# One-core attention with routed experts: route in pieces over the next batch, a new order of the attention steps, the first expert's split on GpSimd, and six shared PSUM banks

## The chip, the cores and the metric

The kernel runs on one core of a Trainium2 chip. The metric is the device time of one execution in microseconds. The engines are TensorE (PE, with its weight loads PEld), VectorE (DVE), ScalarE (ACT), GpSimd (POOL) and SyncE (SP), which here only issues DMAs. Each takes its own instructions in order and waits on semaphores.

## The reference

Attention over 8 batches, 8 heads, 576 positions and head size 64, with a bias that depends on the position; the result, 4608 tokens of 512 values, goes through a layer of 8 experts of which each token takes one.

```python
scores = scale * np.matmul(q, k.transpose(0, 1, 3, 2)) + bias      # bias: a small net of the relative position
attn = np.exp(scores - max); attn = attn / (np.sum(attn, axis=-1, keepdims=True) + 1e-09)
x = np.matmul(attn, v)                                             # as (4608, 512)
logits = x @ w_gate; expert_idx = np.argmax(logits, axis=1); gate_w = softmax(logits)[expert_idx]
for e in range(E):
    h = np.maximum(x[expert_idx == e] @ w1[e], 0.0)
    out[expert_idx == e] = gate_w * (h @ w2[e])
```

With the inputs of this case the experts get 0, 1728, 638, 0, 1090, 576, 576 and 0 tokens. Expert 1 has the most, after six batches as after seven.

## The kernel before

**Attention.** The heads of a batch form four pairs; a pair's 576 query rows are five tiles (four of 128 rows, a tail of 64). The first ten tiles run while the bias is still built. The other 150 are steps of a list that `attend_units` writes out by hand: each operation of a step gets a key, the step's number plus an offset from the tables `LATER` and `PRODUCTS`, and all are sorted by key and issued in that order under `manual_schedule`, so the order of PE, DVE and ACT is fixed by these tables. A step is: `scores` (PE, twelve matmuls into two PSUM tiles of the pool `ps_s`, which has two), `biased` (DVE, one for each head: adds the bias and finds the row minimum), `weights` (ACT, the exponential, whose row sums go to the tile `r`), `turn` (PE transposes, in two parts, each into two of the three tiles of the pool `ps_t`) and `turned` (copies to SBUF, part on ACT, part on DVE). Tiles are joined to units, [0, 1] and [2, 3, 4] of a pair. For a unit follow `values` (PE, five pieces of four matmul instructions into the single tile of `ps_o`), `values_out` (ACT), `rows` (PE, turns back and forms the gate's logits, in a `ps_t` tile), `divided` (DVE, 1e-9 and reciprocal of the sums) and `rows_out` (DVE, scales rows and logits out of the `ps_t` tile). For the next pairs `first_part` (ACT) and `second_part` (DVE) split q and k in a high and a low half. The last two pairs run as ten units of one tile each.

**Route.** Once a batch is through, `route` (a generator with seven yields and so eight pieces) picks each token's expert, counts ranks (on GpSimd, then two pairs of matmuls), and scatters the rows to DRAM by GpSimd's indirect DMAs. `advance(1)` runs one piece; the list has one in every step.

**Experts.** `first_expert` picks the fullest expert so far; `load_first` reads its first weights; `split_first` splits them in high and low halves (four chunks, high by a DVE cast, low by a GpSimd subtraction) and loads the second weights into the same raw tiles. The first block of 384 tokens (`tokens`, `first_product`) starts at the end of the attention. `run` then splits the second weights (ACT, DVE) and goes through the experts; each runs one arm of a switch, with blocks of up to 384 tokens. A block is `first_product` (PE at line 705, ACT relu at 695, DVE low half at 696, PSUM tiles from `ps_h`, three) and `second_product` (lines 741 to 743, DVE at 745, indirect DMA at 746, PSUM tiles from `ps_y`, three). `fetch` loads the next expert's eight chunks, w1 in the chunks 0 to 3 and w2 in 4 to 7, and splits w2 on GpSimd. Outside the hand-written order a planner with a model of the costs sets the order in each engine.

Of the kernel before, what the change touches and what calls it, by code (L numbers as in the profile page):

```python
# [48 lines left out]
    "S": 0.000, "St": 0.040, "W0": 0.497, "W1": 0.498, "Wt": 0.839, "X0": 0.575, "X1": 1.291, "Xt": 0.930,  # L49
    "R1": 1.085, "R2": 1.921, "R1t": 1.872, "E1a": 1.506, "E1b": 1.546, "E2a": 1.922, "E2b": 1.937, "E1at": 2.076,  # L50
    "E1bt": 2.107, "hi0": 1.250, "lo0": 4.000, "hi1": -0.245, "lo1": 1.364, "raw": -2.445, "v": -2.500, "route": -0.261,
}
PRODUCTS = {
    "two": ((2.690, 2.691, 4.592, 4.689, 4.690), 4.691, 6.523, 2.285, 6.524),
    "three": ((2.108, 2.109, 2.110, 2.111, 3.123), 3.548, 5.123, 2.096, 5.923),
    "one": ((2.700,) * 5, 2.800, 4.133, 4.033, 4.933),
}
AW = max(sum(QN[qt] for qt in qts) for qts in UNITS)
LEAD, RATE = 15, 4

# [27 lines left out]
def attention(tc, ctx, q, kt, vm, ltab, bcst, gate, gt, cm, cmat, ival, tail0, pcst, bias, xs, plan, moe):  # L88
# [154 lines left out]

    def divided(un):

        r, m, tail = un["r"], 2 * len(un["qts"]), QN[un["qts"][-1]] < P
        nc.vector.tensor_scalar(out=r[:, :m - tail], in0=r[:, :m - tail], scalar1=1e-9, scalar2=None, op0=ALU.add)
        nc.vector.reciprocal(out=r[:, :m - tail], in_=r[:, :m - tail])
        if tail:
            nc.vector.tensor_copy(out=r[:64, m - 1:m], in_=r[64:, m - 2:m - 1])  # L250
# [41 lines left out]
    for t in r_tiles:  # L292
        nc.gpsimd.memset(t, 0.0)
    r_tiles = itertools.cycle(r_tiles)

    def attend(b, pr, qt):
# [18 lines left out]
        with tc.manual_schedule(engines=PE):  # L315
            rows(un)
        divided(un)
        rows_out(un)

    def attend_units(units, ops):  # L320
# [8 lines left out]
        for b, pr, qts in units:  # L329
# [3 lines left out]
            for i, (qt, st) in enumerate(zip(qts, sts)):  # L333
# [24 lines left out]
                at(k + LATER["route"], lambda: advance(1))  # L358
            when, o, x, d, y = PRODUCTS[("one", "two", "three")[len(qts) - 1]]
# [4 lines left out]
            at(last + x, lambda un=un: rows(un))  # L364
            at(last + d, lambda un=un: divided(un))
            at(last + y, lambda un=un: rows_out(un))
            if pr == NPAIR - 1 and qts[-1] == QT - 1:
                at(last + y + .01, lambda b=b: pending.append(route(b)))
            if p not in begun:
                begun.append(p)  # L370
# [26 lines left out]
    def route(b):  # L397
# [42 lines left out]
        nc.scalar.activation(out=lg, in_=lg, func=AF.Exp)  # L440
        g = rp_.tile([P, QT], F32, name="g")
# [164 lines left out]
    ops += [((B - 1, 3, 4), key, token_part) for key in (-2., 2.953, 2.963, 2.973, 2.983)]  # L606
# [14 lines left out]
class Experts:  # L621
# [163 lines left out]
    def run(self, ctx):  # L785
# [17 lines left out]
        for c in range(NC):  # L803
            self.split(NC + c, 0, raw=self.wraw[c])
# [129 lines left out]
```

## Time and profile before

| | us |
|---|---|
| median of three runs | 1101.14 (1099.69 to 1104.77) |
| the profiled execution, own time | 1104.94 |
| its span, first to last instruction | 1103.0 |
| mean granted TensorE clock | 0.967 |
| PE, DVE, ACT, POOL busy | 1008.5, 653.7, 560.9, 172.0 |

The span has a stage of attention with the bias being built (to about 107 us), a long even stage of attention (to 534 us), the last two pairs (to 602 us), the first block of the first expert (to 642 us), the rest of the experts (to 1082 us) and an end of 20.6 us after the last matmul. Times in the profile are microseconds from the start of the span, and a line number is that of the listing above. A matmul's end is modelled, so neighbours overlap; the distance between two starts tells the pace.

### The profile page before, as it was taken

The page shows a single profiled execution, that of the slowest core. Times are in us where ns is not written, and L with a number is a line of the kernel's source. Part 1 is how long each engine was busy: PE and PEld are TensorE (multiplying, and loading weights), DVE is VectorE, ACT ScalarE, POOL GpSimd, SP SyncE. Part 2 cuts the span into 40 slices and gives each one's busy share as a digit, 9 for nine tenths or more (in the row PEclk, how much of TensorE's full clock was granted, in tenths as well). Part 3 has the DMA queues.
Part 4 walks back from the last instruction along what each step waited for, and adds up shares of the span by engine and source line. Part 5 has one row for each costly group of instructions (what it writes and reads, how often), then busy time and mean ns, then how long its engine had stood idle before and what let it go on. Part 6 is the DMA issues. An engine that isn't in the chain of part 4 may idle for free. (4 is left out here: it accounts for less than half of the span.)

```text
span 1103.0 us, 24830 instructions
## 1 busy us (share of the span) xinstructions
PE 1008.5 (91%) x9564; PEld 799.5 (72%) x9564; DVE 653.7 (59%) x1794; ACT 560.9 (51%) x1371; POOL 172.0 (16%) x235
## 2 busy tenths in 40 slices
PE   7888899999999999999995999999898999898892
PEld 3445676777777776767674888889787899786791
DVE  7677588888888888888887523224232323223140
ACT  6776587888888887878864111113122123022130
POOL 0000002002020202011032224000410500151320
PEclk9899799999999999999998899999999999999896
DMA  8444122223232323223133273003416102606000
GB/s 246 120 110 98 46 61 93 80 60 114 60 103 70 104 71 102 64 63 107 49 133 106 70 280 117 24 27 106 162 49 243 49 10 83 211 23 205 36 20 30
DMA packets 39046, 104.89 MB, mean 95 GB/s; under 512 B 4835, under 2 KB 5347, under 8 KB 38755
## 3 DMA queue, kind: packets, MB, share of 16 engines
q1 hardware_dynamic: 32642, 83.01, 24.7%
q0 software_dynamic: 5920, 18.95, 4.7%
q8 instruction: 91, 1.49, 0.6%
q14 instruction: 105, 0.85, 0.2%
q10 hardware_dynamic: 288, 0.59, 0.2%
HBM read 72.97 MB, written 23.97 MB: 88 GB/s over the span
## 5 line engine op out<-in xcount | busy, mean ns | idle before, releaser
L190 ACT ACTIVATE a<-t,mn 128x576 f32<-128x576 f32 x288 | 224.2, 778 | 62.9 <-DVE mn L182 59.4
L705 PE MATMUL psh<-bias,bias 128*128 128x384 f32 (+2 forms) x1248 | 207.8, 323 | 22.1 <-issue 13.5
L182 DVE CUSTOM_DVE_ANT_0 t<-s,bias 128x576 f32<-128x576 f32 x288 | 207.6, 753 | 32.5 <-PE s L173 26.8
L705 PEld LDWEIGHTS psh<-bias,bias 128*128 128x128 f32 x1248 | 198.8, 195 | 29.1 <-issue 15.2
L228 PE MATMUL o<-at,v 128*64 128x256 f32 (+3 forms) x1520 | 186.3, 380 | 14.6 <-DVE at L215 12.7
L695 ACT ACTIVATE bias<-psh 128x384 fp32r<-128x384 f32 (+2 forms) x104 | 46.5, 451 | 263.8 <-PE psh L705 263.5
L207 PEld LDWEIGHTS tps<-cm,a 64*128 64x128 f32 (+1 forms) x2624 | 116.6, 140 | 70.6 <-issue 34.8
L207 PE MATMUL tps<-cm,a 64*128 64x64 f32 (+1 forms) x2624 | 147.5, 233 | 11.5 <-DVE at L218 8.7
L228 PEld LDWEIGHTS o<-at,v 128*64 128x64 f32 x1520 | 92.5, 138 | 63.7 <-DVE at L215 12.3
L218 ACT COPY at<-tps 128x320 f32<-128x320 f32 (+1 forms) x312 | 116.4, 392 | 41.6 <-PE tps L207 37.1
L696 DVE SCALAR_TENSOR_TENSOR bias<-psh,bias 128x384 fp32r<-128x384 f32 (+2 forms) x104 | 51.6, 504 | 110.5 <-ACT bias L695 108.9
L218 DVE COPY at<-tps 128x320 f32<-128x320 f32 (+1 forms) x200 | 92.7, 464 | 26.2 <-PE tps L207 24.7
L173 PE MATMUL s<-kh,qh 64*128 64x288 f32 x512 | 95.7, 338 | 5.1 <-ACT ob L562 3.9
L741 PE MATMUL psy<-w2h,bias 128*128 128x512 f32 (+1 forms) x224 | 88.6, 398 | 0.0
L742 PE MATMUL psy<-w2l,bias 128*128 128x512 f32 (+1 forms) x224 | 88.1, 396 | 0.0
L743 PE MATMUL psy<-w2h,bias 128*128 128x512 f32 (+1 forms) x224 | 88.0, 396 | 0.0
L746 POOL DMA_INDIRECT out<-y,ids x38 | 37.3, 981 | 303.2 <-DVE y L745 270.8
L745 DVE TENSOR_SCALAR y<-psy,g 128x512 f32<-128x512 f32 (+1 forms) x38 | 28.4, 747 | 94.6 <-PE psy L743 94.6
L173 PE MATMUL s<-kh,ql 64*128 64x288 f32 x512 | 83.1, 298 | 0.0
L173 PE MATMUL s<-kl,qh 64*128 64x288 f32 x512 | 82.0, 296 | 0.0
L680 ACT CAST bias<-tps 128x384 fp32r<-128x384 f32 (+2 forms) x60 | 24.6, 461 | 87.0 <-PE tps L678 77.0
L419 POOL TENSOR_TENSOR cs<-cs,oh 128x8 f32<-128x8 f32 x40 | 8.1, 202 | 376.8 <-DVE oh L414 374.3
(168 smaller groups left out, 1511.0 us busy)
## 6 DMA issues: line engine op xcount, KB each, us to landing
bias<-in_wl SPq DMA_DIRECT2D x28, 512.0 KB, 3.4
qn<-in_q SPq DMA_DIRECT2D x32, 320.0 KB, 2.9
v<-in_vm SPq DMA_DIRECT2D x32, 320.0 KB, 3.1
wr<-in_wl SPq DMA_DIRECT2D x20, 512.0 KB, 8.3
xg<-xs SPq DMA_DIRECT2D x12, 774.0 KB, 8.9
kn<-in_kt SPq DMA_DIRECT2D x32, 288.0 KB, 2.8
bias<-ob SPq DMA_DIRECT2D x32, 288.0 KB, 3.5
xs<-in_none SPq DMA_DIRECT2D x6, 774.0 KB, 5.0
```

The costliest lines, as they stand in the source:

```text
L173: nc.tensor.matmul(ss[hh][:, hf, :SH], x[d, q0:q0 + P], y[d, hf * SH:hf * SH + SH], start=i == 0, stop=i == 2)
L182: nc.vector.tensor_tensor_reduce(out=t, in0=st["s"][hh][:, :, :SH], in1=bt.rearrange("p (a c) -> p a c", a=2), op0=ALU.add, op1=ALU.min, s ...
L190: nc.scalar.activation(out=st["a"][:, hh * S:(hh + 1) * S], in_=st["t"][hh].rearrange("p a c -> p (a c)"), func=AF.Exp, bias=st["mn"][:, h ...
L207: nc.tensor.transpose(ts[half][:m, i * 64:i * 64 + 64], a[d, k0[half]:k0[half] + m], ident[d, d])
L218: copy(out=at[:, first:first + len(places), c0 + 64 * half:c0 + 64 * half + 64], in_=t[:, :64 * len(places)].rearrange("p (c q) -> p c q", ...
L228: nc.tensor.matmul(un["o"][d, :N], v[:, c, d], at[:, c if c == 4 else 5 * hh + c, :N], start=i == 0, stop=i == 4, skip_group_check=True)
L695: nc.scalar.activation(out=hi, in_=ps, func=AF.Relu)
L696: nc.vector.scalar_tensor_tensor(out=lo, in0=ps, scalar=0.0, in1=hi.bitcast(F32), op0=ALU.max, op1=ALU.subtract)
L705: nc.tensor.matmul(ps[:, :N], w[c][:, k0:k0 + P], x[kc][:, :N], start=i + kc == 0, stop=i == 2 and kc == KC - 1)
L741: nc.tensor.matmul(ps[:n], a, wh, start=f == 0, stop=False)
L742: nc.tensor.matmul(ps[:n], a, wo, start=False, stop=False)
L743: nc.tensor.matmul(ps[:n], b, wh, start=False, stop=f == FC - 1)
```

## The change

In the attention: new offsets for all steps; the addition of 1e-9 (and the move of the tail's sum) is taken out of `divided` and becomes `raised`, on ACT; the eight pieces of a route stand two steps apart over the next batch (1.3 steps for the seventh batch), from 10.768 steps after the batch's last step, and the exponential of the route ends a piece of its own. `first_expert` now sees the counts of six batches and not of seven. The cast of `split_first` moves from DVE to GpSimd. Among the experts: `first_product` and `second_product` take their PSUM tiles from one pool of six; the low halves of the first expert's second weights are made by GpSimd and not by DVE; `fetch` loads w2 ahead of w1.

```diff
 LATER = {
-    "S": 0.000, "St": 0.040, "W0": 0.497, "W1": 0.498, "Wt": 0.839, "X0": 0.575, "X1": 1.291, "Xt": 0.930,
-    "R1": 1.085, "R2": 1.921, "R1t": 1.872, "E1a": 1.506, "E1b": 1.546, "E2a": 1.922, "E2b": 1.937, "E1at": 2.076,
-    "E1bt": 2.107, "hi0": 1.250, "lo0": 4.000, "hi1": -0.245, "lo1": 1.364, "raw": -2.445, "v": -2.500, "route": -0.261,
+    "S": 0.000, "St": 0.035, "W0": 0.570, "W1": 0.571, "Wt": 0.657, "X0": 0.784, "X1": 1.453, "Xt": 0.778,
+    "R1": 1.176, "R2": 1.888, "R1t": 1.829, "E1a": 1.528, "E1b": 1.596, "E2a": 2.425, "E2b": 2.049, "E1at": 2.290,
+    "E1bt": 2.351, "hi0": -0.113, "lo0": 1.538, "hi1": 1.359, "lo1": 2.762, "raw": -2.313, "v": -2.500, "route": 10.768,
 }
 PRODUCTS = {
-    "two": ((2.690, 2.691, 4.592, 4.689, 4.690), 4.691, 6.523, 2.285, 6.524),
-    "three": ((2.108, 2.109, 2.110, 2.111, 3.123), 3.548, 5.123, 2.096, 5.923),
-    "one": ((2.700,) * 5, 2.800, 4.133, 4.033, 4.933),
+    "two": ((2.742, 3.289, 4.079, 4.736, 4.742), 5.200, 6.742, 3.763, 5.895, 7.000),
+    "three": ((2.495, 2.768, 2.833, 3.408, 3.411), 4.004, 5.412, 3.804, 5.440, 5.933),
+    "one": ((3.014,) * 5, 3.114, 4.421, 3.104, 4.322, 4.943),
 }
+ROUTE_STEP = (2., 1.3)
+    def raised(un):
+        r, m, tail = un["r"], 2 * len(un["qts"]), QN[un["qts"][-1]] < P
+        if tail:
+            nc.scalar.activation(out=r[:64, m - 1:m], in_=r[64:, m - 2:m - 1], func=AF.Identity, bias=tiny[64:], scale=1.0)
+        nc.scalar.activation(out=r[:, :m - tail], in_=r[:, :m - tail], func=AF.Identity, bias=tiny, scale=1.0)
+
     def divided(un):
-        r, m, tail = un["r"], 2 * len(un["qts"]), QN[un["qts"][-1]] < P
-        nc.vector.tensor_scalar(out=r[:, :m - tail], in0=r[:, :m - tail], scalar1=1e-9, scalar2=None, op0=ALU.add)
-        nc.vector.reciprocal(out=r[:, :m - tail], in_=r[:, :m - tail])
-        if tail:
-            nc.vector.tensor_copy(out=r[:64, m - 1:m], in_=r[64:, m - 2:m - 1])
+        r, m = un["r"], 2 * len(un["qts"])
+        nc.vector.reciprocal(out=r[:, :m], in_=r[:, :m])
...
-                at(k + LATER["route"], lambda: advance(1))
...
                 at(last + y + .01, lambda b=b: pending.append(route(b)))
+                if b < B - 1:
+                    for i in range(8):
+                        at(last + LATER["route"] + i * ROUTE_STEP[b == B - 2], lambda: advance(1))
...
         nc.scalar.activation(out=lg, in_=lg, func=AF.Exp)
+        yield
...
-            self.split(c, None, self.nc.vector.tensor_copy, self.nc.gpsimd)
+            self.split(c, None, self.nc.gpsimd.tensor_copy, self.nc.gpsimd)
...
-            ps = self.ps_y.tile([P, DM], F32, name="psy")
+            ps = self.ps_p.tile([P, 512], F32, name="psp")
...
-                self.first_product(nt, lambda: self.ps_h.tile([P, 512], F32, name="psh"))
+                self.first_product(nt, lambda: self.ps_p.tile([P, 512], F32, name="psp"))
...
-        self.ps_h = ctx.enter_context(tc.tile_pool(name="ps_h", bufs=3, space=PSUM))
+        self.ps_p = ctx.enter_context(tc.tile_pool(name="ps_p", bufs=6, space=PSUM))
...
-        self.ps_y = ctx.enter_context(tc.tile_pool(name="ps_y", bufs=3, space=PSUM))
...
-            self.split(NC + c, 0, raw=self.wraw[c])
+            self.split(NC + c, 0, lo_by=nc.gpsimd, raw=self.wraw[c])
...
-                    for c in range(2 * NC):
+                    for c in (*range(NC, 2 * NC), *range(NC)):
```

## Rows read from the trace of the kernel before

**Rows 1.** Windows: stage, us; busy PE, PEld, DVE, ACT, POOL; clock, DMA share, GB/s.
```profile
151.06:534.33 383.27, 373.63 (x4928) 276.90 (x4929) 333.11 (x1022) 320.02 (x857) 40.37 (x96) 1.00 0.28 83
534.33:602.14 67.81, 54.96 (x776) 43.95 (x776) 54.76 (x165) 39.51 (x109) 17.48 (x19) 0.92 0.33 107
642.20:1082.40 440.20, 418.09 (x2269) 371.47 (x2267) 137.68 (x253) 87.86 (x180) 104.20 (x77) 0.98 0.29 102
```
**Rows 2.** Timeline, one pair of the even stage, PE: start us, us, operation, [idle <-releaser].
```profile
321.21 0.38 PE L173 MATMUL s<-kh,qh 64*128 64x288 f32 x2
...
323.94 0.38 PE L173 MATMUL s<-kh,qh 64*128 64x288 f32 x2
...
325.15 2.37 PE L228 MATMUL o<-at,v 128*64 128x320 f32 x16
...
327.79 0.38 PE L173 MATMUL s<-kh,qh 64*128 64x288 f32 x2
...
330.53 0.38 PE L173 MATMUL s<-kh,qh 64*128 64x288 f32 x2
...
333.24 0.40 PE L165 MATMUL s<-kh,qh 128*128 128x288 f32 x1
...
335.85 0.38 PE L173 MATMUL s<-kh,qh 64*128 64x288 f32 x2
```
**Rows 3.** Timeline, DVE: the last `rows_out` of three pairs, a route between them.
```profile
350.29 0.56 DVE L261 TENSOR_TENSOR xrow<-tps,r 128x384 f32<-128x384 f32 x1 [0.35 <-PE tps L242]
...
366.81 0.55 DVE L261 TENSOR_TENSOR xrow<-tps,r 128x384 f32<-128x384 f32 x1
...
382.32 0.56 DVE L261 TENSOR_TENSOR xrow<-tps,r 128x384 f32<-128x384 f32 x1 [0.35 <-PE tps L242]
```
**Rows 4.** Lines by form, 200 to 500 us: count | busy us, mean ns | idle before.
```profile
L247 DVE TENSOR_SCALAR r<-r 128x5 f32<-128x5 f32 x20 | 3.1, 156 | 0.0
...
L440 ACT ACTIVATE lgsum<-lgsum 128x40 f32<-128x40 f32 x5 | 1.2, 236 | 0.0
```
**Rows 5.** Timeline around the first expert's split: DVE, POOL, PE.
```profile
575.51 6.78 DVE L665 CAST bias<-bias 128x1024 fp32r<-128x1024 f32 x4
582.21 2.30 DVE L247 TENSOR_SCALAR r<-r 128x2 f32<-128x2 f32 x1
584.55 0.17 DVE L248 RECIPROCAL r<-r 128x2 f32<-128x2 f32 x1
...
576.28 10.52 POOL L666 TENSOR_TENSOR bias<-bias,bias 128x1024 fp32r<-128x1024 f32 x4 [12.37 <-DVE bias L665]
...
586.50 0.69 PE L207 MATMUL tps<-cm,a 64*128 64x64 f32 x8 [8.65 <-DVE at L218]
```
**Rows 6.** Timeline, POOL, 640 to 685 us: a later expert's split of one chunk.
```profile
663.34 1.03 POOL L665 CAST w2h3b<-wr 128x1024 fp32r<-128x1024 f32 x1
664.34 2.38 POOL L666 TENSOR_TENSOR w2l1b<-wr,w2h1b 128x1024 fp32r<-128x1024 f32 x1
```
**Rows 7.** Timeline where attention hands over to the first block: SP, PE, DVE.
```profile
587.36 0.40 SPq L673 DMA_DIRECT2D bias<-xs  x1
...
602.14 1.20 PE L678 MATMUL tps<-cm,bias 128*128 128x128 f32 x9
606.71 1.56 PE L705 MATMUL s<-bias,bias 128*128 128x384 f32 x6 [3.36 <-ACT bias L680]
...
603.47 4.63 DVE L666 TENSOR_TENSOR w2l<-bias,w2h 128x1024 fp32r<-128x1024 f32 x4 [1.80 <-ACT w2h L665]
```
**Rows 8.** The page's DMA issues: count, KB each, median us to landing.
```profile
xg<-xs SPq DMA_DIRECT2D x12, 774.0 KB, 8.9
```
**Rows 9.** Waits over the span: us in total, times, longest.
```profile
PE psh L705 <- DVE bias L696: 8.1, 4, 2.7
```
**Rows 10.** Timeline, PE, an expert's first product after a switch of arms.
```profile
779.58 6.48 PE L705 MATMUL psh<-bias,bias 128*128 128x384 f32 x36 [0.98 <-issue]
788.50 3.91 PE L705 MATMUL psh<-bias,bias 128*128 128x384 f32 x12 [2.43 <-DVE bias L696]
```

## What the rows say of the change

> **What bounds the kernel now.** I read the windows by stage first [rows 1]: the reader is to see that in the even stage of attention, 383.27 us for 25 pairs, no engine is full. DVE is busy 333.11 us (87%), ACT 320.02 (83%), and PE's 373.63 is a sum of modelled, overlapping matmuls. So the order of three nearly full engines sets the pace, and not one of them. Among the experts PE is busy 418.09 of 440.20 us at a clock of 0.98, DVE 31%: there only PE's gaps can be won. The stage between them, the last two pairs, has PE busy 54.96 of 67.81 us at a clock of 0.92.
>
> Next comes the timeline of one pair [rows 2]. Starts of scores stand at 321.21, 323.94, 327.79, 330.53, 333.24 and 335.85: a pair takes 14.64 us, in steps of 2.73, 3.85, 2.74, 2.71 and 2.61. Four steps are alike although PE has different work in them: scores fill both tiles of their pool and DVE has to read both before the next scores, and this loop is the floor. The long one is different: PE runs 16 value matmuls in it, 2.37 us without a break. Then the pairs with a route [rows 3]: 350.29 to 366.81 is 16.52 us, to 382.32 another 15.51, so 2.75 us over two plain pairs. The stage as a whole agrees: 383.27 less 25 times 14.64 (366.0) leaves 17.3 us for six routes, 2.9 each.
>
> Last, the single stalls. At 575.51 DVE begins the casts of the first expert's weights; they take 6.78 us, the small sum behind them 2.30, and PE stands 8.65 us [rows 5]. Among the experts PE waits four times, 8.1 us in all, for DVE to free a tile of the first product [rows 9].
>
> **The change part by part.** The profiled execution took 1104.94 us (span 1103.0 and 1.9 around it), 3.8 over the median of 1101.14. I sum against 1104.94 and take off 3.8 at the end.
>
> *Order of the steps.* By the new tables, PE has in the long step three pieces (12 matmuls) of the three-tile unit's values where it had four; a piece is 2.37 / 4 = 0.59 us [rows 2]. The next step has two where it had one. Of the two-tile unit's pieces the step behind that gives one to the tail's step. Long step: -0.7 (the piece and part of the wait of the transposes behind it; bounds -0.4 and -0.9). Next step: it is at the floor, so a piece costs between 0 (it fits into PE's wait) and 0.59; I take +0.3, the middle, as nothing shows PE's free time there. The two last steps: the tail's scores need one PSUM tile and not two, so the fourth can fall under the floor by up to 0.5, and the fifth gains a piece (0 to +0.5); I take -0.1 for both. Sum -0.5 us a pair, bounds -0.8 and +0.2. There are 28 pairs in the list, of which the first overlaps the bias's last stores: 27 x 0.5 = 13.5 us won, from -5 to +22.
>
> *The addition on ACT.* DVE loses a sum for each unit (0.156 us in [rows 4]) and the tail's copy, some 0.46 us a pair; ACT gains three small activations, at 0.236 at most [rows 4] 0.7 us a pair. ACT then has 320.02 / 383.27 x 14.64 + 0.7 = 12.9 of 14.1 us, so it still has room. What waits on it: only the reciprocal, which the tables put more than a step behind. Row sums come from ACT itself, so the new activation waits for nothing. I cost it at nothing beside the order above, which is what its 0.46 us on DVE makes possible; if ACT's room is gone, it costs up to 0.7 a pair, which the bound of the order takes in.
>
> *Route in pieces.* Eight pieces stood one step apart, in 1.6 pairs; they now stand two apart, in 3.2. DVE's idle time is 14.64 x 0.13 = 1.9 us a pair: 3.0 us beside the pieces before, 6.1 after, and 1.5 more for the sums taken away. Before, the ranks' matmuls also stood in PE's queue one step behind DVE's comparison and GpSimd's five sums; now two steps lie between. A piece still costs when it falls where DVE is late. I take 10 of the 17.3 us as won (bounds 0 and 17.3), and 1 of the seventh route, which moves into the single-tile units.
>
> *First split on GpSimd.* The casts leave DVE, and no DVE work there waits for them. That removes PE's 8.65 us. PE's clock of 0.92 in the stage means 0.08 / 0.5 x 67.81 = 10.8 us at 1.2 GHz, of which about 2.2 lie in work behind the stall: another 1.1. Against it: GpSimd now takes 4 x (1.03 + 2.38) = 13.6 us [rows 6] and not 10.52, though it may start on landed weights without DVE, while the second weights' and then the tokens' loads queue behind it on SP. The tokens' load was issued at 587.36 [rows 7]; by the median of 8.9 [rows 8] it lands by 596.3, and PE, 9.7 earlier, would want it at 602.14 - 9.7 = 592.4. So 0 to 3.8 us turn into a wait for that load; I take 1, since the weights' loads ahead of it make up the median. And DVE can wait for GpSimd: the third and fourth cast took most of the 6.78 us and the sum 2.30 where 0.156 is usual, all while GpSimd subtracted [rows 4, 5]; the reciprocal, 0.17, ran through. In the new order two or three of the seventh route's operations fall into the 13.6 us; 1 us. Net 7.7, from 3 to 9.7.
>
> The Trainium skill ("SBUF — State Buffer", section "SBUF: two separate sides") says that DVE, when it works over two ports or with two SBUF inputs, and GpSimd hold a shared port pair by turns, each for a whole instruction. The rows above agree for the sum (2.30 us against 0.156); the case of two SBUF inputs no row here shows. It speaks against moving work to GpSimd, and what it would do is the third rival below.
>
> *Second weights' low halves on GpSimd.* DVE was held 4.63 us from 603.47 while the tokens' low halves waited, but PE's 3.36 us at that place is ACT's [rows 7], whose casts stay. I take 1 us won, up to 3.4 if the planner also moves those casts, and down to -3 if GpSimd's 4 x 2.38 = 9.5 us, ahead of the last route's sums, holds PE at the ranks.
>
> *Six shared banks.* At 779.58 PE runs three results of 12 matmuls, 6.48 us, and stops 2.43 us because DVE is still at the switch; the next 12 take 3.91 and not 6.48 / 3 = 2.16, as the clock has fallen [rows 10]. With six tiles PE has three more results, 6.5 us, ahead: enough for the longest wait of 2.7 [rows 9]. 8.1 us for the four waits and 3 for the clock: 11 won. At worst the second product's partial results hold banks when they are wanted, and 4 remain.
>
> *w2 ahead of w1.* GpSimd, which splits w2, is busy 104.20 of 440.20 us [rows 1], and the second product wants it only a block later. Nothing, within 2 us.
>
> Sum: 13.5 + 10 + 1 + 7.7 + 1 + 11 = 44.2. 1104.9 - 44.2 = 1060.7, less 3.8: 1057 us.
>
> **The rivals.** *First, attention gains nothing (chance 0.2).* The new order only moves its waits, because the floor of 2.7 is what counts, and the route's pieces cost what they did. For it: four of five steps stand at the floor. Against: 3.85 does not. Left are 7.7 + 1 + 11: 1101.1 - 19.7 = 1081.
>
> *Second, slower (0.07).* The pool of the transposes has three tiles, and `rows` holds one until `rows_out` has read it. In the new order `rows_out` of the two-tile unit stands on DVE behind the low half of k, in a route's batch behind a piece too, and PE's next transposes want its tile. If PE stands there for 1.1 us in each pair and no route is hidden, attention is 28 x 1.1 = 31 us slower and the whole 1081 + 31 = 1112. It decides from 0.7 us a pair (19.7 / 28). Against it: DVE has 1.9 us idle a pair.
>
> *Third, the lock (0.08).* Every DVE operation with two SBUF inputs, not the sums alone, waits up to a GpSimd instruction of 2.38 us while GpSimd splits. Three in the seventh route and some four in the first block, half of it on the path: 7 x 2.38 / 2 = 8 us of the gain go, 1065. For it: the 2.30 [rows 5].
>
> *Fourth, the shared banks do not do what they say (0.03):* the planner gives them to the second product and PE still stops: 1068.
>
> **How the numbers follow.** The forecast has 0.62, 1057, its own range 1040 to 1073. The range for 8 in 10 reaches from 1040 (gains near all upper bounds, 61 us) to 1085 (the first rival and 4 us); outside lie the slower rival and some of each edge. About 0.5% is what a measurement of this kernel can tell from no change, so faster means under 1095.6: forecast, first, third and fourth rival nearly whole, 0.89; within it 0.04; slower 0.07.
>
> **What would show it.** The order: scores' starts in a plain pair with the longest step near 3.1 and a pair near 14.1. Route: pairs behind a batch's end within 0.6 us of the others. Split: no wait of PE over 4 us near the last pairs, casts at line 665 on POOL. Banks: no wait of the first product for line 696 over 0.5 us. The prediction is wrong if a pair takes 14.6 or more, if PE waits for the tokens' load by more than 4 us, or if DVE's small sums in the split's 13.6 us take over 2 us each.

## The result and the profile after

The changed kernel takes 1069.84 us (median of four runs, 1069.25 to 1071.44); the kernel before took 1100.71 on the same chip. The ratio is 0.9715, with a 95% interval from 0.9688 to 0.9742: 30.9 us won where 44 were forecast. The profiled execution took 1071.44 us, its span 1069.6, the mean clock was 0.977. Of the experiments below, those that undo one part ran on a chip like this one (before: 1100.3), but for the order of the chunks; that run and the other two groups ran on chips where the kernel before itself takes 1128.5 us, so that their times are set against before, and their stages against each other.

Line numbers are up by 12 or so: scores 174 (tail 166), transposes 208, values 229, `rows_out` 266, the route's sums 430 and ranks 434, split 677 and 678, token casts 692, first product 717, its casts and low halves 707 and 708, second product 753 to 755, its scaling 757.

**The stages.** Windows of the kernel after: even stage, last two pairs, from the tokens' transposes to the first second product, from there to the last matmul. Columns as in [rows 1].

```profile
151.02:524.40 373.38, 372.72 (x4928) 276.44 (x4928) 320.57 (x946) 334.18 (x932) 42.16 (x96) 1.00 0.27 85
524.40:591.36 66.96, 57.60 (x757) 43.79 (x757) 44.14 (x147) 40.67 (x123) 20.02 (x23) 0.95 0.32 106
591.36:617.11 25.75, 21.64 (x142) 19.18 (x140) 16.41 (x56) 10.80 (x23) 13.10 (x16) 1.00 0.03 12
617.11:1049.11 432.00, 425.81 (x2320) 378.36 (x2320) 150.09 (x267) 86.83 (x180) 106.52 (x81) 0.99 0.32 110
```

The last two stages of the kernel before, cut at the same events:

```profile
602.14:623.64 21.50, 16.79 (x87) 14.84 (x85) 13.50 (x47) 7.73 (x14) 1.01 (x5) 0.84 0.00 1
623.64:1082.40 458.76, 436.65 (x2357) 387.57 (x2356) 143.77 (x283) 89.83 (x184) 109.78 (x87) 0.98 0.30 104
```

| stage | before | after | won | forecast |
|---|---|---|---|---|
| even stage | 383.27 [rows 1] | 373.38 | 9.9 | 22.5 (order 25 x 0.5, route 10) |
| last two pairs | 67.81 [rows 1] | 66.96 | 0.9 | 9.7 (order 1, route 1, split 7.7) |
| handover and experts | 480.26 | 457.75 | 22.5 | 12 (low halves 1, banks 11) |

The sum, 33.3, is the difference of the spans within 0.1. Attention gave a third of what was forecast, the experts nearly twice. The border between handover and experts moves with the PSUM tiles (22.38 us lie ahead of it with two pools, below), so only the sum of the two is compared.

**The even stage.** Starts of scores in a pair of after (timeline, PE, as in [rows 2]):

```profile
330.54 0.38 PE L174 MATMUL s<-kh,qh 64*128 64x288 f32 x2
...
333.28 0.38 PE L174 MATMUL s<-kh,qh 64*128 64x288 f32 x2
...
336.59 0.38 PE L174 MATMUL s<-kh,qh 64*128 64x288 f32 x2
...
339.86 0.38 PE L174 MATMUL s<-kh,qh 64*128 64x288 f32 x2
...
342.27 0.40 PE L166 MATMUL s<-kh,qh 128*128 128x288 f32 x1
...
345.31 0.38 PE L174 MATMUL s<-kh,qh 64*128 64x288 f32 x2
```

The steps are 2.74, 3.31, 3.27, 2.41 and 3.04, together 14.77, where [rows 2] give 2.73, 3.85, 2.74, 2.71 and 2.61, together 14.64. The long step did get shorter, by 0.54, and its neighbour longer by 0.53. Added up by groups, from start to start in the two timelines, TensorE's scores take 4.57 us in the pair before and 4.60 in after, its values 5.36 and 5.40, its `rows` 1.48 and 1.43 and its transposes 3.23 and 3.34. The groups take nearly the same in either order, and they fill both pairs.

Beside it, the last `rows_out` of the pairs over a batch's end (timeline, DVE, as in [rows 3]):

```profile
345.09 0.56 DVE L266 TENSOR_TENSOR xrow<-tps,r 128x384 f32<-128x384 f32 x1 [0.85 <-PE tps L243]
...
359.85 0.56 DVE L266 TENSOR_TENSOR xrow<-tps,r 128x384 f32<-128x384 f32 x1
...
374.61 0.56 DVE L266 TENSOR_TENSOR xrow<-tps,r 128x384 f32<-128x384 f32 x1 [0.58 <-PE tps L243]
...
390.12 0.56 DVE L266 TENSOR_TENSOR xrow<-tps,r 128x384 f32<-128x384 f32 x1 [0.73 <-PE tps L243]
```

Plain pairs (those without a route's matmuls; small operations of a route on DVE or GpSimd may lie in them) take 14.76, and one in each batch 15.51: a route costs 0.75 us where [rows 3] gave 2.75.

**The last two pairs.** The 8.65 us of [rows 5] are gone, and another wait stands in their place (timeline, POOL and PE):

```profile
551.01 2.37 POOL L678 TENSOR_TENSOR bias<-bias,bias 128x1024 fp32r<-128x1024 f32 x1
553.35 0.19 POOL L430 TENSOR_TENSOR cs<-cs,oh 128x8 f32<-128x8 f32 x1
553.51 4.64 POOL L678 TENSOR_TENSOR bias<-bias,bias 128x1024 fp32r<-128x1024 f32 x2
558.12 1.02 POOL L430 TENSOR_TENSOR cs<-cs,oh 128x8 f32<-128x8 f32 x4
...
559.19 0.66 PE L434 MATMUL tps<-cs,cm 128*128 128x48 f32 x2 [5.09 <-POOL cs L430]
```

Windows of the wait and of what follows it:

```profile
554.10:559.19 5.09, 0.00 (x0) 0.00 (x0) 0.42 (x1) 2.22 (x7) 4.80 (x6) 0.98 0.85 306
559.19:566.20 7.01, 6.94 (x62) 6.07 (x64) 2.79 (x10) 1.27 (x5) 1.04 (x1) 0.53 0.25 79
```

The seventh route's five sums on GpSimd are 0.2 us each, but the planner put one subtraction of the split ahead of the first of them and two between it and the other four. TensorE stands for the ranks, and then runs 7 us at a clock of 0.53.

**Handover and experts.** ScalarE's tokens' casts and its casts of the second weights, and two small operations of the last route on DVE beside GpSimd's subtractions (timelines):

```profile
591.94 1.37 ACT L692 CAST bias<-tps 128x384 fp32r<-128x384 f32 x3
...
595.08 3.89 ACT L677 CAST w2h<-bias 128x1024 fp32r<-128x1024 f32 x4
...
601.27 2.08 DVE L419 TENSOR_TENSOR oh<-lgsum,mx 128x40 f32<-128x40 f32 x1
603.38 2.31 DVE L420 TENSOR_TENSOR oh<-oh,ivt 128x40 f32<-128x40 f32 x1
...
596.21 9.42 POOL L678 TENSOR_TENSOR w2l<-bias,w2h 128x1024 fp32r<-128x1024 f32 x4 [10.01 <-ACT w2h L677]
```

The tokens' casts now stand ahead of the weights', so the 3.36 us of [rows 7] are gone. The two DVE operations have two operands in SBUF and ran while GpSimd subtracted; the first ends at 603.35 and the second at 605.69, where GpSimd's third and fourth subtraction end (603.29 and 605.63). TensorE's waits from the first second product on (total, times, longest):

```profile
PE psp L717 <- issue: 3.4, 1, 3.4
PE psp L717 <- DVE y L757: 2.8, 3, 0.9
```

Of the waits for the low halves, [rows 9], none is left here. The waits that the trace gives to "issue", 13.5 us in four before, 0.98 of them in [rows 10], are down to one of 3.4. In the first block, whose products stand in other tiles than the six (`s`), TensorE does wait for the low halves, where before had one wait of 1.0 (window 591.36 to 617.11):

```profile
PE s L717 <- DVE bias L708: 2.9, 2, 1.6
```

### The profile page after: what moved, and what is told of

It is laid out like the page before. It is cut to its first block, busy times and chain, and to the rows that moved or that the text cites. A ratio compares the mean times of both kernels' runs of the same rounds, so it can differ in the third digit from the quotient of the medians.

```text
span 1069.6 us, 24922 instructions
## 1 busy us (share of the span) xinstructions
PE 1003.5 (94%) x9564; PEld 793.2 (74%) x9564; DVE 637.4 (60%) x1678; ACT 579.7 (54%) x1479; POOL 185.2 (17%) x244
## 4 chain that ended last, share of the span: by engine, by line
PE 47%; issue 26%; DMA 14%; POOL 5%; ACT 3%; DVE 3%; another core or an unknown queue 1%; POOLq 0%; SPq 0%; DVEq 0%; ACTq 0%
PE o L229 16%; DMA out<-y,ids 12%; PE tps L208 11%; PE s L174 10%; PE tps L243 4%; PE s L572 3%; PE s L166 3%; POOL out L758 2%; DMA bias<-ob 1%; ACT a L191 1%; PE s L717 1%; DVE t L183 1%; ACT ob L574 1%; POOL bias L678 1%; POOL w2l L678 1%
## 5 line engine op out<-in xcount | busy, mean ns | idle before, releaser
L183 DVE CUSTOM_DVE_ANT_0 t<-s,bias 128x576 f32<-128x576 f32 x288 | 207.6, 754 | 41.1 <-PE s L174 30.9
L717 PE MATMUL psp<-bias,bias 128*128 128x384 f32 (+2 forms) x1248 | 197.2, 319 | 6.2 <-issue 3.4
L717 PEld LDWEIGHTS psp<-bias,bias 128*128 128x128 f32 x1248 | 194.0, 192 | 9.4 <-issue 7.9
L229 PE MATMUL o<-at,v 128*64 128x256 f32 (+3 forms) x1520 | 193.7, 384 | 3.0 <-DVE at L216 2.0
L707 ACT ACTIVATE bias<-psp 128x384 fp32r<-128x384 f32 (+2 forms) x104 | 46.4, 450 | 221.0 <-PE psp L717 217.8
L708 DVE SCALAR_TENSOR_TENSOR bias<-psp,bias 128x384 fp32r<-128x384 f32 (+2 forms) x104 | 51.0, 504 | 86.5 <-ACT bias L707 84.4
L219 DVE COPY at<-tps 128x320 f32<-128x320 f32 (+1 forms) x200 | 90.0, 459 | 10.6 <-PE tps L208 10.1
L757 DVE TENSOR_SCALAR y<-psp,g 128x512 f32<-128x512 f32 (+1 forms) x38 | 28.5, 749 | 107.2 <-PE psp L755 107.2
L753 PE MATMUL psp<-w2h,bias 128*128 128x512 f32 (+1 forms) x224 | 89.8, 401 | 1.2 <-DVE planf L508 1.2
L754 PE MATMUL psp<-w2l,bias 128*128 128x512 f32 (+1 forms) x224 | 88.8, 396 | 0.0
L755 PE MATMUL psp<-w2h,bias 128*128 128x512 f32 (+1 forms) x224 | 88.8, 396 | 0.0
L572 PE MATMUL s<-h,bc 128*32 128x288 f32 x576 | 55.5, 436 | 12.0 <-DVE mn L183 4.4
```

The lines of the kernel that those rows point to most:

```text
L183: nc.vector.tensor_tensor_reduce(out=t, in0=st["s"][hh][:, :, :SH], in1=bt.rearrange("p (a c) -> p a c", a=2), op0=ALU.add, op1=ALU.min, s ...
L219: copy(out=at[:, first:first + len(places), c0 + 64 * half:c0 + 64 * half + 64], in_=t[:, :64 * len(places)].rearrange("p (c q) -> p c q", ...
L229: nc.tensor.matmul(un["o"][d, :N], v[:, c, d], at[:, c if c == 4 else 5 * hh + c, :N], start=i == 0, stop=i == 4, skip_group_check=True)
L572: nc.tensor.matmul(ps[32 * j:32 * j + 32, hf, :SH], w2bd, hs[j][:, hf * SH:(hf + 1) * SH], start=True, stop=True)
L717: nc.tensor.matmul(ps[:, :N], w[c][:, k0:k0 + P], x[kc][:, :N], start=i + kc == 0, stop=i == 2 and kc == KC - 1)
L753: nc.tensor.matmul(ps[:n], a, wh, start=f == 0, stop=False)
```

## The experiments

**One part undone at a time, on one chip.** The measure for the three that follow is the changed kernel itself.

> The changed kernel itself, as the measure for the three that each undo one part of it on the same chip. By its first runs 0.9715 of the kernel before. Its rows should stand again: 14.76 us in a plain pair, 5.1 us of TensorE's wait for the seventh route's sums, 0.94 us three times and 3.4 once among the experts.

Measured: 1068.97 us (1065.79 to 1069.19), 0.9696 of before (0.9652 to 0.9741). Plain pairs 14.76, last two pairs 66.66, handover and experts 25.76 + 432.00.

*Two pools of three banks.*

```diff
-        self.ps_p = ctx.enter_context(tc.tile_pool(name="ps_p", bufs=6, space=PSUM))
+        self.ps_h = ctx.enter_context(tc.tile_pool(name="ps_h", bufs=3, space=PSUM))
+        self.ps_y = ctx.enter_context(tc.tile_pool(name="ps_y", bufs=3, space=PSUM))
```

> The kernel after with two pools of three PSUM tiles for the two products, as before. Theory of the prediction (with three tiles TensorE stops when VectorE is still at the switch between experts, 8.1 us in four waits for the low halves and 3 in clock): 8 to 11 us slower than the kernel after. Rival one (the four waits without a named releaser, 0.98, 3.15, 1.48 and 7.88 us in the kernel before, which after shows as 0.94, 0.94, 0.94 and 3.38, belong to the three tiles too): 8 + 7 + 3, some 18 us slower, and both kinds of wait are in its trace at the switches. Rival two (these four went with the order of the weights' chunks): the waits for the low halves come back, the others stay at 0.94 and 3.4, 8 to 11 us.

Measured: 1087.48 us, 0.9882 of before (0.9836 to 0.9928), 18.5 over after. TensorE's waits from the first second product on:

```profile
PE psh L717 <- DVE bias L708: 14.2, 4, 4.1
PE psh L717 <- issue: 3.7, 1, 3.7
```

The window around one of them:

```profile
774.00:790.00 16.00, 15.12 (x76) 14.58 (x77) 7.53 (x13) 3.08 (x7) 13.51 (x8) 0.89 0.57 174
```

The handover and the experts take 22.38 + 452.07 = 474.5 us and not 457.8: the banks are worth 16.7 us. That is the size of rival one. Where before has a nameless wait at a switch and one for the low halves 8 to 9 us behind it (0.98 and 2.43 in [rows 10], 3.4 to 4.4 together at three switches), this version has one wait of 3.8 to 4.1, given to line 708; a fourth wait for this line takes 2.3. So three of the four nameless waits belong to the three tiles. The fourth, 7.9 us in before, does not: it is 3.7 here and 3.4 in after, and no run undoes what shortened it. All waits of the stage make up 18.8 - 7.4 = 11.4 us; the clock behind three of them (0.89 for 16 us, 0.92 for 21, 0.91 for 18) makes 0.11 x 16 + 0.08 x 21 + 0.09 x 18 = 5 us.

*The casts of the first split on DVE.*

```diff
-            self.split(c, None, self.nc.gpsimd.tensor_copy, self.nc.gpsimd)
+            self.split(c, None, self.nc.vector.tensor_copy, self.nc.gpsimd)
```

> The kernel after with the four casts of the first expert's first weights on VectorE again; GpSimd keeps the subtractions. Theory of the prediction: TensorE stands 8.65 us behind the casts, and 1.1 us of clock and a late tokens' load go with it, 7.7 us slower than after. Rival, from the trace of after: after already stands 5.09 us, because the subtractions are ahead of the seventh route's sums on GpSimd; with the casts on VectorE the subtractions come later and that wait goes, so only 8.65 - 5.09 = 3.6 us slower, or none where the casts fall into VectorE's idle time (5.72 us behind the wait).

Measured: 1072.32 us, 0.9732 of before (0.9684 to 0.9779). TensorE's waits in the last two pairs:

```profile
PE tps L208 <- DVE at L219: 4.7, 2, 4.2
```

The wait for GpSimd's sums is gone, and one of 4.2 behind DVE's casts stands instead. The stage takes 68.07 us against 66.66: moving the casts to GpSimd was worth 1.4 us (0.9 to 1.7 against the four profiled executions with the casts on GpSimd in this place, 66.36 to 67.18). The rest of the 3.4 us between the medians lies within the intervals; the profiled executions already differ by 3.2 us in the stage that builds the bias, which both kernels share.

*The low halves of the second weights on DVE.*

```diff
-            self.split(NC + c, 0, lo_by=nc.gpsimd, raw=self.wraw[c])
+            self.split(NC + c, 0, raw=self.wraw[c])
```

> The kernel after with the four low halves of the first expert's second weights on VectorE again. Theory of the prediction (a gain of 1 us by GpSimd, bounds -3 and +3.4): 1 us slower than after, with VectorE held some 4.6 us ahead of the tokens' low halves or of the small operations of the last route. Rival (the lock: two operations of the last route with two SBUF inputs took 2.08 and 2.31 us in after where 0.20 is usual, while GpSimd subtracted): these two take 0.2 each, TensorE's waits of 1.34, 1.60 and 1.17 us behind them shrink to under 1 us each, and this version is 2 to 4 us faster than after.

Measured: 1066.63 us, 0.9691 of before (0.9648 to 0.9734). The same two operations of the last route (timeline, DVE):

```profile
600.13 0.20 DVE L419 TENSOR_TENSOR oh<-lgsum,mx 128x40 f32<-128x40 f32 x1
600.37 0.20 DVE L420 TENSOR_TENSOR oh<-oh,ivt 128x40 f32<-128x40 f32 x1
```

They take 0.20 each without GpSimd's subtractions beside them: the lock is real. On the path it is worth little: handover and experts take 26.21 + 431.07 = 457.3 us against 457.8. So neither 1 us of gain nor 2 to 4 of loss is to be seen in these stages. The medians differ by 2.3 us; in the profiled executions as much lies behind the last matmul (18.9 us here, 21.3 in the changed kernel), where neither version differs, and the intervals of the two ratios overlap.

*The chunks of the next expert in the old order* (on another chip).

```diff
-                    for c in (*range(NC, 2 * NC), *range(NC)):
+                    for c in range(2 * NC):
```

> The kernel after with the chunks of the next expert's first weights loaded ahead of its second weights, as before. The stage from the first second product to the last matmul took 458.75 us before, 432.00 in after, and 452.07 with two pools of three banks, so some 6.7 of the 26.7 us are not the banks'. Theory of the prediction (the order of the chunks is worth nothing, within 2 us): 430 to 434 us in this stage, the time within 2 us of after. Rival (the second weights' late landing held the switches, the 6.7 us are the chunks'): some 438 us in this stage, and the wait of 3.4 us without a named releaser at the last switch grows, or others like it appear.

Measured: 1106.62 us, 0.9813 of before on that chip (0.9762 to 0.9865); the stage of the experts 434.00 us against 432.00, with one more wait of 2.4 us at a switch. The order of the chunks is worth 2 us, the edge of what was allowed; the rival's 438 are out. As a whole this version cannot be set against after, which was not run on this chip: its pairs beside a scatter take 17 to 20 us (last section). It is the nearest to after that ran on such a chip, and it won 1.9% there and not 2.9%.

**GpSimd in the order of the text.**

```diff
-    with tc.manual_schedule(engines={..., mybir.EngineType.Activation}):
+    with tc.manual_schedule(engines={..., mybir.EngineType.Activation, mybir.EngineType.Pool}):
```

> The kernel after with GpSimd too held to the order of the text in attention: the five sums of the seventh route then stand ahead of the first expert's split. Theory (the 5.09 us for which TensorE stood at 559.19 come from three subtractions of the split that the planner had put ahead of these sums): that wait goes, and with it some of the clock's fall behind it (566 - 560 us at half speed, up to 2.5 us): 1069.8 - 5 to 7.5, 1062 to 1065. Rival (the split, now some 5 to 10 us later on GpSimd, delays the second weights' loads, the tokens' load behind them on SP and so the handover): TensorE waits instead ahead of the tokens' transposes, and the time stays at 1068 to 1072.

Measured: 1072.09 us (1070.59 to 1072.87), 0.9487 of before on that chip (0.9446 to 0.9528). GpSimd's row (timeline):

```profile
555.36 1.31 POOL L430 TENSOR_TENSOR cs<-cs,oh 128x8 f32<-128x8 f32 x5 [25.83 <-DVE oh L425]
556.61 1.04 POOL L677 CAST bias<-bias 128x1024 fp32r<-128x1024 f32 x1
```

The window of the last two pairs:

```profile
530.07:592.53 62.46, 55.67 (x756) 41.79 (x757) 45.37 (x147) 41.81 (x126) 20.37 (x24) 1.00 0.34 113
```

The five sums stand together ahead of the split, the wait for them is gone, the clock is 1.00 throughout, and the stage takes 62.46 us where after takes 66.66 to 66.96: 4.2 us or more, as the theory had it. Against the casts on DVE (68.07 us) the split on GpSimd is then worth 5.6. No later wait takes its place; the handover is 25.85 us. The absolute time can't be held against 1062 to 1065, as the chip is a slower one.

**What sets the pair.** Four versions were built to find out which engine holds a plain pair, and two with the order of before.

```diff
-            for i in range(5):
+            for i in (0, 1, 2, 4):
                 at(last + when[i], lambda un=un, i=i: values(un, i))
```

> The kernel after without the fourth of five pieces of each unit's value product (128 of the 576 keys are left out of the weighted sum; everything else is computed). The piece is 4 matmul rows for each unit: by the rows of one pair 0.54 to 0.59 us in the three-tile unit and 0.48 in the two-tile unit, some 1.05 us a pair. Rival (TensorE's own stream bounds the pair): a plain pair falls from 14.76 by the whole 1.05 to about 13.7, and the even stage by 25 times that. Theory of the prediction (the loop scores, two sums, scores is the floor of the steps near 2.7): pieces in steps at the floor cost nothing, so a pair falls by at most half of it, to 14.2 or more.

```diff
+        nc.vector.tensor_scalar(out=spare[0], in0=spare[0], scalar1=1.0, scalar2=None, op0=ALU.mult)
```

> The kernel after with one more small VectorE operation (128 x 16, in place, nothing reads it) behind each of the nine sums with the bias of a pair: by the 0.156 us of a 128 x 10 operation some 1.4 us more on VectorE in each pair of 14.76, where it has 2.0 to 2.8 idle. Theory of the prediction (the loop scores, two sums, scores is the floor): the operation behind the first sum of a tile lies in the loop, at least 5 x 0.156 = 0.8 us a pair, 15.5. Rival (TensorE's own stream bounds the pair): the pair stays at 14.76, within 0.1.

The next has the first of these edits and `divided` as it was before.

> The kernel after without the fourth of five pieces of each unit's value product (128 of the 576 keys are left out of the weighted sum) and with the addition and the tail's copy on VectorE as before. Without the piece alone a pair fell only from 14.76 to 14.70 to 14.73, although 1.05 us of matmuls were gone, and 1.4 us more on VectorE alone cost nothing. Theory one (ScalarE's queue is the second bound, 13.1 us busy and 0.9 of it the additions): with both relieved a pair falls well under 14.5, by up to 0.9 us. Theory two (a loop over several engines, scores, sum, exponential, transposes, copy, fixed by the key tables, is the second bound): a pair stays at 14.6 to 14.7.

The fourth has GpSimd in the order of the text, `divided` as before, and other keys for the two-tile unit's values:

```diff
-    "two": ((2.742, 3.289, 4.079, 4.736, 4.742), 5.200, ...
+    "two": ((2.742, 3.289, 3.290, 4.736, 4.742), 5.200, ...
```

> The kernel after with GpSimd held to the order of the text, with the addition and the tail's copy on VectorE, and with the second to fourth pieces of the two-tile unit's values next to each other, so that TensorE changes between kinds of matmuls once less in a pair, as before. Theory (TensorE's stream and ScalarE's both stand within 0.1 us of the pair, and each is relieved): a plain pair takes 14.65 or less, 2.7 us over the even stage; the wait of 4.6 to 5.1 us for the seventh route's sums is gone, the stage of the last two pairs is at 62.5 us and not 66.7. The whole is some 7 us faster than after, near 1062. Rival (the fixed loop sets the pair): a plain pair stays at 14.76, and only the 4 to 5 us of the last pairs are won, 1064 to 1065.

Measured, by the window of one plain pair each (columns as in [rows 1]; POOL's 1.00 in two of them is a route's sums). After:

```profile
345.09:359.85 14.76, 14.76 (x200) 10.95 (x200) 13.04 (x36) 13.28 (x38) 0.00 (x0) 1.00 0.28 76
```

Less values (1099.72 us in one run, before 1128.67):

```profile
163.27:177.99 14.72, 14.54 (x191) 10.61 (x192) 12.95 (x36) 13.11 (x38) 0.00 (x0) 1.00 0.23 66
```

More DVE (1101.09 us in one run, before 1128.67):

```profile
246.25:261.00 14.75, 14.75 (x200) 10.95 (x198) 13.48 (x50) 13.13 (x38) 1.00 (x5) 1.00 0.24 67
```

The added operation costs less than its 0.17 us (timeline, DVE):

```profile
152.50 0.76 DVE L184 CUSTOM_DVE_ANT_0 t<-s,bias 128x576 f32<-128x576 f32 x1 [0.33 <-PE s L175]
...
153.19 0.17 DVE L188 TENSOR_SCALAR spare<-spare 128x16 f32<-128x16 f32 x1
153.26 0.75 DVE L184 CUSTOM_DVE_ANT_0 t<-s,bias 128x576 f32<-128x576 f32 x1
```

The second sum starts 0.76 us behind the first, in after 0.68 (346.49 to 347.17): the nine operations delay DVE by some 0.08 each, 0.7 us a pair and not 1.4, and the theory's five by 0.4 and not 0.8.

Less values and less ScalarE (1096.07 us in one run, before 1128.48):

```profile
240.16:254.36 14.20, 14.10 (x192) 10.32 (x186) 13.25 (x44) 11.95 (x35) 1.01 (x5) 1.00 0.25 69
```

The combined version:

```profile
161.97:176.97 15.00, 15.00 (x198) 11.04 (x200) 13.49 (x39) 12.60 (x36) 0.00 (x0) 1.00 0.21 64
```

Taking 1.05 us of matmuls away wins 0.04; adding 0.7 us to DVE costs nothing; taking both matmuls and ScalarE's additions away wins 0.56 (14.20 here, 14.51 in other plain pairs). So DVE's sums don't hold the pair, and TensorE alone doesn't either: behind it, within 0.05 us, stands a chain in which ScalarE's work counts. The first test speaks against its rival (13.7) and leaves the loop standing (14.2 or more); the second speaks against the loop, which even with 0.4 us would have given some 15.1. The combined version shows a trap as well. It runs the same matmuls as after and before, in 15.00, 14.76 and 14.64 us, and in all three PE's row is busy without a gap. Added up by the starts, its scores take 4.84 us where before has 4.57 (one group of twelve takes 1.14 and not 0.88) and its transposes 3.33 where before has 3.23: there the 0.36 us are, most likely waits too short for the row. The weight loads (PEld) do stand idle in each of these pairs, by up to 0.5 us; in before's (321.21 to 335.85) 0.6 us until ScalarE's copies and 0.5 until its exponentials. Whether these set the pace isn't shown. Its new keys also missed their aim, as the pieces still stand in three groups (of 4, 8 and 8 matmuls, in after 4, 4 and 12). Its last two pairs took 61.60 us, like those of the version before it; the whole, 1095.55, is 0.9713 of before on its chip (0.9668 to 0.9758), and 0.99 of the one with the chunks in the old order beside it.

*The old order* (tables of before, the addition on ScalarE with a key directly ahead of the reciprocal).

```diff
-    "S": 0.000, "St": 0.035, "W0": 0.570, ...
+    "S": 0.000, "St": 0.040, "W0": 0.497, ...
-    "three": ((2.495, 2.768, 2.833, 3.408, 3.411), 4.004, 5.412, 3.804, 5.440, 5.933),
+    "three": ((2.108, 2.109, 2.110, 2.111, 3.123), 3.548, 5.123, 2.095, 2.096, 5.923),
```

> The kernel after with the key tables of before (the order of scores, sums, exponentials, transposes and value pieces); the addition stays on ScalarE, with a key just ahead of the reciprocal, and the route stays two steps apart. Theory of the prediction (a loop over the two tiles of scores and DVE's reads sets the pace, and the new tables shorten it by 0.5 us a pair): this version is 27 x 0.5 = 13.5 us slower than after, near 1083. Rival (TensorE's own instructions fill the pair: 14.64 of 14.64 us in a plain pair before, 14.76 of 14.76 in after, so the tables are worth only the switches between kinds of matmuls): a plain pair takes 14.65 again, this version is 25 x 0.1 = 2.5 us faster than after in the even stage, near 1067, and a route's batch still costs only about 0.75 us, since the pieces stay spread.

Measured: 1138.34 us, 1.0086 of before (1.0058 to 1.0114), against both theories. TensorE's waits in its pairs from 153 to 220 us:

```profile
PE o L229 <- DVE at L216: 3.6, 4, 0.9
```

A plain pair takes 15.57. The reciprocal on DVE waits for the addition on ScalarE right ahead of it, the tail's copies stand behind the reciprocal, and TensorE's values wait for them, 0.9 us in each pair. The key was badly chosen for a test of the order; but it measures what the prediction's clause "the tables put more than a step behind" is worth.

*The old order and the old sum* (the same tables, `divided` as before).

> The kernel after with the key tables of before and with the addition and the tail's copy on VectorE as before; the route's pieces stay two steps apart, and the split and the banks as in after. Theory of the prediction (the new tables shorten the pair by 0.5 us): a plain pair takes 14.64 us only if they don't; with the theory the even stage of 25 pairs is 13 us longer than in after. Rival (the new tables and the addition on ScalarE gain nothing, and the even stage won its 9.9 us by the route's pieces alone): a plain pair is back at 14.65 where after has 14.76, one pair in each batch some 0.75 us longer, the even stage 370 to 371 us where after has 373.4, and the whole 2 to 3 us faster than after, but for the handover, where the casts on ScalarE may cost 3.4 us again.

Measured: 1111.85 us, 0.9843 of before (0.9798 to 0.9888), on a chip whose pairs behind a scatter stall (below). The first batch has no scatter yet, and on this chip the version with the chunks in the old order takes 59.77 us for its four pairs, after on its own chip 59.78 (timeline, DVE, `rows_out`):

```profile
150.57 0.56 DVE L262 TENSOR_TENSOR xrow<-tps,r 128x384 f32<-128x384 f32 x1 [0.35 <-PE tps L243]
165.21 0.56 DVE L262 TENSOR_TENSOR xrow<-tps,r 128x384 f32<-128x384 f32 x1 [0.35 <-PE tps L243]
180.29 0.56 DVE L262 TENSOR_TENSOR xrow<-tps,r 128x384 f32<-128x384 f32 x1
194.89 0.55 DVE L262 TENSOR_TENSOR xrow<-tps,r 128x384 f32<-128x384 f32 x1
210.16 0.56 DVE L262 TENSOR_TENSOR xrow<-tps,r 128x384 f32<-128x384 f32 x1
```

Four pairs with a whole route take 59.59 us: 59.78 in after (3 x 14.76 + 15.50), and 61.33 before (14.66, 16.51, 15.52, 14.64). Spreading the route alone wins 1.74 us a batch, and the new tables with the addition on ScalarE lose 0.2. As in before, this version's handover has a wait of 3.35 us for ScalarE's casts. The combined version, with the new tables and the old sum, has none, so the new tables moved these casts in after, and not GpSimd.

## Why the prediction came out as it did

**The order of the steps: wrong, and by all of it** (13.5 won; measured 0.2 us a batch lost). The first half of the step was right: the piece that leaves the long step takes 0.54 us with it (forecast 0.7). What failed is the next sentence, that the step which receives the piece "is at the floor, so a piece costs between 0 and 0.59; I take +0.3". It cost 0.53, and the last two steps, put at -0.1, came to -0.30 and +0.43. Four equal steps were read as a loop in which TensorE waits; by the starts in the timeline each was filled by other matmuls of TensorE, and their likeness was chance. The misreading starts in the first paragraph, which sets PE's 373.63 of 383.27 us aside as a sum of overlapping matmuls. Busy time counts no moment twice (a plain pair has 14.64 of 14.64), so TensorE was idle for 9.6 us where the forecast for this stage won 22.5. One view of the trace of before would have spoken against it too, TensorE's waits in the even stage:

```profile
PE o L228 <- DVE at L215: 8.9, 12, 0.9
```

That is all in 383 us, and the twelve waits stand two to each of the six routes: no plain pair has one. So a new order could win next to nothing there unless it also shortened what TensorE and ScalarE do. The experiments narrow this and don't close it: which chain holds the pair once TensorE is relieved stays open, except that DVE's sums aren't in it and ScalarE's work is.

**The addition on ScalarE: within its bound, not measured apart.** No run undoes it alone; with the new tables it loses 0.2 us a batch, where the bound was 0.7 a pair. The old-order run shows 0.9 a pair where the tables leave it no room.

**The route in pieces: right** (10 forecast of 17.3). 1.74 us x 6 = 10.4 by the version with the old tables. Of the 0.75 us left the four rank matmuls take 0.57 on TensorE (377.24 to 377.81 in after); I had left 7.3 without saying for what.

**The first split on GpSimd: wrong place** (7.7 and 1 for the seventh route; the stage won 0.9). DVE's casts were rightly seen as the cause of 8.65 us, and the loads behind the split on SP as the risk; the tokens' load then cost nothing. The queue that I didn't walk was GpSimd's own: five sums of 0.2 us, for which the ranks wait, were in it. The conflict is one of place and not of load: with the same work in the order of the text the stage is 4.2 us shorter. That is half of the 8.8 us missing; in that version neither the wait nor the clock's fall is left, and the stage still wins 5.3 of 9.7, so the other half has a cause that no run shows.

**The low halves on GpSimd: no gain** (1 forecast, bounds -3 and +3.4); the run that undoes it is 0.5 shorter in these stages. The 3.36 us of [rows 7] went all the same, by the new order of ScalarE's casts, which stood in the forecast only as its upper bound. So of the 22.5 us of handover and experts 16.7 are the banks' and 2 the chunks', by the runs that undo them. For the other 3.8 the casts' 3.4 are the likeliest, but no run undoes these alone: the version with the old tables and the old sum, where the wait is back, takes 465.2 us in these stages and not 457.8.

**Six shared banks: right mechanism, too small** (11; measured 16.7). The term counted the waits whose releaser was named, 8.1 us, and left out the 13.5 us marked "issue" beside them, one of which stands in [rows 10]. With three banks three of these four are part of the waits at the switches; with six, three of 0.9 are left there, and the last one, 3.4, isn't the banks'. The clock behind them was put at 3 and is some 5.

**The rivals.** The first, that attention gains nothing, was half of what happened: the order gained nothing, but the route its 10, which leads from that rival's 1081 to near 1070. That the time fell into the stated range owes something to luck: 21.4 us of attention's gains were missing, and 10.5 that the forecast did not have came among the experts. The second didn't occur: TensorE is idle for 0.7 us of the even stage. The fourth is refuted by the banks' run. The third, the lock, is there: 2.08 and 2.31 us where 0.20 is usual. The Trainium skill ("SBUF — State Buffer", section "SBUF: two separate sides") counts DVE operations with two SBUF inputs among those that share a port pair with GpSimd, instruction by instruction; these rows agree, each of the two taking about as long as one of GpSimd's subtractions (2.35 to 2.41) and ending with it. But two operations and not seven met it, and handover and experts differ by no more than 0.5 us without it.

**The marks set beforehand.** "A pair takes 14.6 or more" came true and condemned the order, as said. So did a wait over 4 us near the last pairs. Pairs behind a batch are 0.75 over the others, not 0.6. No first product of the shared pool waits for the low halves; two of the first block do, 1.3 and 1.6 us. TensorE doesn't wait for the tokens' load, and no DVE operation takes over 2 us in the first split; the two that do stand beside the second weights' low halves.

## What to carry to other kernels

Before a new order is priced, add up how long the busiest engine of that stage is idle, and for what. Here it was 9.6 us of 383.3, 8.9 of them beside the routes; 22.5 were forecast and 9.9 came. The row is no exact bound, since it can be full and hide some tenths of a microsecond in a pair, but a forecast of twice the idle time needs a reason. A move to an idle engine is costed by walking that engine's own queue, small operations above all, and by asking who waits for them. Waits without a named releaser that stand at the same switches as named ones may belong to the same resource (three of four did here), which a run that undoes the change can tell.

## What the hardware showed unexpectedly

On the chips where the kernel before takes 1128.5 us, the pair beside each scatter of a batch's rows mostly took 17 to 21 us. The kernel with more DVE, at such a place, in a pair of 19.43 us (timeline, ACT, DVE and PE):

```profile
226.78 0.42 ACT L222 COPY at<-tps 128x320 f32<-128x320 f32 x1 [2.54 <-remote]
226.81 0.49 DVE L222 COPY at<-tps 128x320 f32<-128x320 f32 x1 [3.06 <-remote]
...
227.26 0.47 PE L211 MATMUL tps<-cm,a 64*128 64x64 f32 x4 [2.02 <-ACT at L222]
```

Its windows of the scatter's burst and of what follows:

```profile
220.00:226.00 6.00, 4.52 (x57) 3.32 (x53) 3.58 (x14) 3.35 (x11) 4.68 (x6) 0.97 0.80 279
226.00:231.00 5.00, 3.74 (x35) 2.85 (x35) 1.84 (x7) 3.31 (x9) 0.00 (x0) 0.50 0.14 33
```

In the burst of the scatter (DMA share 0.80) ACT and DVE stop together for something that the trace doesn't name, TensorE behind them, and then it runs at a clock of 0.50. After on the first chip has a like burst (0.83) at the same place and no stop. The version with GpSimd in the order of the text had pairs of 15.1 to 15.4 there, and one of 17.2, and is the fastest relative to before; the combined version has GpSimd in the same order and stalls again, on another chip of this kind, so that order alone doesn't remove the stall, and its cause stays open.
